# Two transformer layers in one kernel: when constants are loaded, early weights are split, and the first query tile's maxima are sent

## Chip, cores and metric

One core of one Trainium2 chip runs the whole program. The metric is device time in microseconds of one execution. The engines are called by the profile's short names as well: TensorE is PE (PEld is its weight load), VectorE is DVE, ScalarE is ACT, GpSimd is POOL, and SyncE, SP, only issues DMA transfers. "SPq" and "ACTq" are the sequencers that issue them.

## The reference

The input `x` has 2048 rows of 640 numbers in float32. Four blocks follow each other, and the two layers use the same weights:

```python
x = x + _A_ref(_layernorm(x, axis=-1), A_wqkv, A_wo)                # attention, 32 heads of 20
x = x + _B_ref(_layernorm(x, axis=-1), B_w1, B_b1, B_w2, B_b2)      # 640 -> 1536 -> 640
x = x + _A_ref(_layernorm(x, axis=-1), A_wqkv, A_wo)
x = x + _B_ref(_layernorm(x, axis=-1), B_w1, B_b1, B_w2, B_b2)
```

`_A_ref` multiplies by `wqkv`, takes `softmax(q k / sqrt(20)) v` over all 2048 keys in each head, and multiplies by `wo`. `_B_ref` is `relu(x w1 + b1)` squared, times `w2`, plus `b2`. The normalisation has no weights of its own.

## The kernel before

Products of activations and weights are made exact to about float32 from three products: each operand is split into a high part, rounded to the matmul's format, and a low part, the remainder (`split_to`: a cast on ScalarE, then a subtraction on VectorE; `split_on_pool`: a copy on ScalarE to a row buffer `r`, then cast and subtraction on GpSimd). Tiles of SBUF come from an arena of 42 slots and a ring of 11 row buffers; a tile that is dropped gives its place to a later one, which waits for the last reader.

Each layer has three stages. `qkv` makes queries, keys and values; `attention` makes scores, exponentials and sums; the rest is the output product and the two products of the dense block. The change lies in `qkv` and in what comes before it.

**Before `qkv`, first layer** (`begin_first`). Four row tiles of x (128 rows each) and four blocks of weight columns (`raw`, in the order `ORDER`) are fetched; two of the row tiles by ScalarE's queue, the rest by SyncE's. Each row tile gets its statistics (`stats`: VectorE, then two small GpSimd operations for the inverse deviation), is normalised and transposed on TensorE against the identity (line 1269), and the five transposed banks are split to `xnT`. The first two weight blocks are split between the third and the fourth row tile. After these instructions stand the constants: a row of ones that goes by `d_one` to `sums_t` and later to the keys, and the biases `b1_t` and `b2_t`. The program has one order per engine and per queue, the order in which it is written out.

**`qkv`.** Forty units (`UNITS`) come first, each a product of one block of 128 query or key columns (`pos`) with 512 rows (`tb`): positions 0 to 3 for each of the four row blocks, then positions 4 to 9. Then 32 chains of values follow (16 row tiles, two halves). The 128 rows of the contraction are cut in two halves of 64, `r` 0 and 1, which TensorE runs beside each other, one half a unit ahead of the other (`work_on`, `product`, line 320). A finished unit leaves PSUM in `end_qk` and is stored to `d_qk` (`later` keeps one store back). Between the products `insert` puts in the matmuls that find the largest score of each query (line 476, reduced on VectorE at line 488), as a small planner with costs for each engine allows; the tiles they need are loaded ahead in `tiles`, `load_q`, `load_k`, `load_kd`. `step_rest` advances normalising and transposing of the next rows (`front`, line 395). Two dictionaries, `early` and `late`, hold calls that run ahead of or behind a unit of a given number: fetches and splits of weights in the first layer; in the second, where split weights come back from DRAM, loads of `w_qk` and of the seven pieces of `w_v` (`wv<-d_wv`).

**The first query tile.** When all maxima of tile 0 are there, `end_group` reduces and transposes them (`mrows_max`, `mrows`), which GpSimd splits to `mr`, and writes them to DRAM (`d_m<-mr`); at the next insertion `mrows_load` reads them back as extra rows of the query tile (`q<-d_m`). The list `later_rows` joins the two. SyncE issues everything in order, and each of its transfers waits until its source is written.

Of the kernel before, what the change touches and what calls it, by code (L numbers as in the profile page):

```python
# [16 lines left out]
P = 128  # L17
# [4 lines left out]
DH = 20  # L22
# [17 lines left out]
def tile_layers(  # L40
# [249 lines left out]

    mark_t = cpool.tile([1, 2], F32, name="mark_t")
    nc.vector.memset(mark_t, 0.0)

    def after(later, earlier):
        tc.add_manual_dep(
# [32 lines left out]
    def end_qk(pos, tb, dst):  # L328
        ev = slot([P, 2, QB], F32R, "ev")
        which, jj = divmod(ORDER[pos], 5)  # L330
        rows = slice(jj * P, (jj + 1) * P)
        kd = None
        if which and pos < FIRST:


            if not keys:
                keys.update(of=slot([P, 2, QB], F32, "kf"), left=4)
            kf = keys["of"][:, jj, :]
            r = xtile("r")[:, :QB] if tb % 2 else kf
            if tb:  # L340
                split_on_pool(ev[:, 0, :], ev[:, 1, :], dst, r)
            else:
                split_to(ev[:, 0, :], ev[:, 1, :], dst)
                nc.scalar.copy(r, dst)
            if tb % 2:
                kd = slot([P, 2, QB], F32R, "kd")
                nc.gpsimd.tensor_sub(kf, r, kf)
                pool_hi(kd[:, 0, :], kf)
                pool_lo(kd[:, 1, :], kf, kd[:, 0, :].bitcast(F32))
            keys["left"] -= 1  # L350
            if not keys["left"]:
                keys.clear()
        else:
            (split_on_pool if tb or pos > 3 else split_to)(ev[:, 0, :], ev[:, 1, :], dst)

        def store():
            thrice(d_qk[which, tb, rows], ev, 1 + which)
            if kd is not None:
                thrice(d_kd[tb // 2, rows], kd, 2)

        return store
# [314 lines left out]
    def qkv(first, x_src, rest):  # L676
# [5 lines left out]
        state = {"n": 0, "turn": False, "op": None, "last": "one"}  # L682
        now = {"pe": 0.0, "dve": 0.0, "act": 0.0}
        busy = [0.0] * 8
        early, late, later_rows, soon = {}, {}, [], []
        coming = [y for x in DOUBLE for h in x for y in h if y[2] == "d"]

        def at(when, n, f):
            when.setdefault(n, []).append(f)

        for pos in range(2 if first else FIRST, 10):
            n = UNITS.index((0, pos)) - 5 if pos >= FIRST else pos - 2
            if first:
                if pos >= FIRST:
                    at(early, n - 2, lambda pos=pos: raws.append(raw_cols(wqkv, ORDER[pos])))
                at(late if n else early, n, lambda pos=pos: w_qk.put(
                    raws.pop(0), pos * 10, pos * 10 + KD, KD, nc.scalar.copy,
                    nc.vector.tensor_sub if pos == 2 else pool_lo,
                ))
            else:  # L700
                at(early, n, lambda pos=pos: w_qk.need(pos * 10, pos * 10 + 9))
        for k in range(KD if first else w_v.n):
            n = len(UNITS) - 7 + k
            if first:
                at(early, n - 2, lambda k=k: raws.append(raw_rows(wqkv[:, 2 * D :], k)))
                at(late, n, lambda k=k: w_v.put(
                    raws.pop(0), k * 4, k * 4 + 2, 2, nc.scalar.copy, pool_lo
                ))
            else:
                at(early, n, lambda k=k: w_v.load(k))  # L710
# [16 lines left out]
        def end_group(x):  # L727
            g, qb, c = x
            t = g * NQB + qb
            rest = soon + groups + double + [w[0] for w in work + twos] + [o["w"][0] for o in begun]  # L730
            if t == 0:
                left[t] -= 1 if c in range(4) else 2
                if left[t] == 0:
                    mrows_max(t)
                    mrows(t)
                    later_rows.append(t)
            if (t or left[t]) and all(y[:2] != (g, qb) for y in rest):
                del q_t[t]
            use = {(y[0], y[2]) for y in rest + coming}
            use |= {(h, 2 * "de".index(y)) for h, y in use if y not in range(4)}  # L740
            for y in [y for y in k_t if y[0] == g and y not in use]:
                if g < 2 or y[1] not in range(4):
                    del k_t[y]
# [59 lines left out]
        def insert(par):  # L803


            while later_rows:
                mrows_load(later_rows.pop())
            op = state["op"]
            if bool(op) != bool(par):
                return False  # L810
            if now["pe"] < max(busy[b] for b in ps_q.coming(1)):
                return False
            if state["turn"] and not par:
                if now["pe"] < max(busy[b] for b in ps_q.coming(2)):
                    return False
                now["pe"] += 1.2
                for spot in ps_q.coming(2):
                    takes("act", 0.6, spot)
                    takes("dve", 0.7, spot)
                step_rest()  # L820
                return False
            if not op:
                op = state["op"] = choose()
                if not op:
                    return False
                state["last"] = op["kind"]
            single(op, par)
            if par:
                state["op"] = None
            return True  # L830
# [10 lines left out]
        def end(n):  # L841

            what, a, b = chains[n]["of"]
            dst = chains[n].pop("dst")
            now["act"] = max(now["act"], now["pe"]) + 0.6
            if what == "qk":
                pending.append(end_qk(b, a, dst))
                if b >= FIRST and a == NQB - 1 or n == 4 * FIRST - 1:
                    w_qk.past(b * 10 + 9, w_qk.got)
                return  # L850
            f = end_v(a, b, dst)
            if f:
                later(1)
                pending.append(f)
                if a == 10:
                    load_v(0, 0)
                if a == 12:
                    for c in range(4):
                        assert (0, c) not in k_t
                        load_k(0, c, True)  # L860
                    load_q(1)
                if a == 14:
                    for c in (1, 3):
                        if (2, c) not in k_t:
                            load_k(2, c, True)
                if a % 4 == 3:
                    del xt_[a // 4]
# [374 lines left out]
    def second():  # L1242
# [7 lines left out]
            yield  # L1250
        yield from front(3, d_x[1], ps_q, 2, (1, 3))

    def begin_first():

        rows = []
        for i in range(4):
            t = xtile("x")
            dma((nc.sync, nc.scalar)[i % 2], t, x_in[i * P : (i + 1) * P, :])
            rows.append(t)
        for pos in range(FIRST):  # L1260
            raws.append(raw_cols(wqkv, ORDER[pos]))
        yield
        dsts = [ps_all("xt") for _ in range(KD)]
        mvs = []

        def turn(i):
            normalise(nc.vector if i else nc.gpsimd, rows[i], mvs[i])
            for k in range(KD):
                nc.tensor.transpose(
                    dsts[k][:, i * P : (i + 1) * P], rows[i][:, k * P : (k + 1) * P], ident  # L1270
                )

        for i in range(4):
            mvs.append(stats(rows[i]))
            if i:
                turn(i - 1)
        for pos in range(2):
            w_qk.put(raws.pop(0), pos * 10, pos * 10 + KD, KD, nc.scalar.copy, pool_lo)
        turn(3)
        rows.clear()  # L1280
        steps = [front(tb, x_in, ps_q, 2, (1, 3)[: tb - 1]) for tb in (1, 2, 3)]
        next(steps[0])
        res = []
        for k in range(KD):
            t = slot([P, 2, QB], F32R, "xnT")
            split_to(t[:, 0, :], t[:, 1, :], dsts[k])
            res.append(t)
            if k == KD - 1:
                xt_[0] = res
            yield 0, False  # L1290
        yield from fronts(steps)
# [1 line left out]
    b2_t = cpool.tile([P, D], F32, name="b2_t")  # L1293
    opening = begin_first()
    next(opening)
    ones = slot([2, QB], F32, "ones")
    nc.vector.memset(ones, 1.0)
    for p in range(2):
        dma(nc.scalar, d_one[:, p, :], ones)
    for h in range(4):  # L1300
        r = 32 * h + DH
        dma(nc.scalar, sums_t[r : r + 1, 32 * h : 32 * h + 32], d_one[0, :1, :32])
    dma(nc.sync, b1_t, b1.rearrange("(f p) -> p f", p=P))
    dma(nc.sync, b2_t, b2.partition_broadcast(P))
    ahead = second()
    layer(True, x_in, d_x[0], d_x[1], opening, ahead)
    layer(False, d_x[1], d_x[2], x_out, ahead, None)
# [28 lines left out]
```

## Time and profile before

| | |
|---|---|
| median of 3 runs | 3685.02 us (3682.33 to 3688.01) |
| the profiled execution | 3682.43 us |
| its span, first to last instruction | 3680.6 us |
| mean granted TensorE clock | 0.996 |
| PE busy | 3624.3 us (98%) |
| DVE, ACT, POOL busy | 2726.4, 2647.6, 804.9 us |

The profile comes from one execution. A timeline row gives start and duration in microseconds, engine, line of the kernel, operation, what it writes and reads, shapes, the number of instructions merged in it and, in brackets, the idle time of the engine before it with what ended it. A waits row gives total, number and longest. A windows row gives the stretch, then busy time and instructions of PE, PEld, DVE, ACT and POOL, the granted clock, and the share and rate of the DMA engines. A row of one tile or line gives shortest, median and longest duration in nanoseconds, first and last start, and shapes.

### The profile page before, as it was taken

How to read it: one execution, taken by the hardware profiler on the slowest of the kernel's cores; microseconds unless marked ns; L12 is line 12 of the kernel's file. 1: busy time of each engine (PE TensorE's matmuls, PEld its weight loads, DVE VectorE, ACT ScalarE, POOL GpSimd, SP SyncE). 2: the span in 40 equal slices, each digit the busy share in tenths (PEclk: the TensorE clock that was granted, in tenths of full speed). 3: DMA queues.
4: the chain of work that ended last, by engine and by line, in shares of the span. 5: the costliest groups of instructions: out<-in, count | busy, mean ns of one | idle time of the engine just before them, and what ended most of it. 6: DMA issues, size and time to landing. Idle time of an engine off the chain costs nothing.

```text
span 3680.6 us, 67584 instructions
## 1 busy us (share of the span) xinstructions
PE 3624.3 (98%) x25738; PEld 2161.0 (59%) x25738; DVE 2726.4 (74%) x5046; ACT 2647.6 (72%) x5202; POOL 804.9 (22%) x894
## 2 busy tenths in 40 slices
PE   7999999999999999999999899999999999999999
PEld 5897334334334336989878874334334333378998
DVE  6877999999999992344567679999999999723443
ACT  2678999999999994122227689999999999941221
POOL 4541344211211121111144202112211211201110
PEclk9999999999999999999999999999999999999999
DMA  7875555323211136411267643232232111373111
GB/s 231 284 251 167 163 145 165 111 65 76 61 46 47 50 100 224 174 44 44 100 225 248 205 148 88 61 81 60 67 79 55 50 49 44 109 251 137 43 49 38
DMA packets 255262, 426.51 MB, mean 116 GB/s; under 512 B 60445, under 2 KB 107293, under 8 KB 254937
## 3 DMA queue, kind: packets, MB, share of 16 engines
q1 hardware_dynamic: 254104, 419.82, 36.9%
q8 instruction: 202, 3.31, 0.4%
q10 hardware_dynamic: 832, 2.37, 0.2%
q14 instruction: 124, 1.01, 0.1%
HBM read 262.20 MB, written 159.88 MB: 115 GB/s over the span
## 4 chain that ended last, share of the span: by engine, by line
PE 94%; DVE 2%; DMA 2%; ACT 1%; SPq 0%; issue 0%; POOL 0%; ACTq 0%; DVEq 0%; POOLq 0%
PE banks L570 28%; PE banks L285 20%; PE banks L558 20%; PE banks L476 15%; PE banks L320 10%; DMA q<-d_qk 1%; DVE h L256 1%; PE banks L1122 0%; PE banks L395 0%; DVE r L1149 0%; ACT h L255 0%; DVE bst L243 0%; SPq L76 0%; ACT r L1148 0%; DVE x L251 0%
## 5 line engine op out<-in xcount | busy, mean ns | idle before, releaser
L565 ACT ACTIVATE e<-banks 128x512 f32<-128x512 f32 x4096 | 2113.3, 604 | 65.6 <-PE banks L476 5.4
L488 DVE TENSOR_REDUCE mx<-banks 128x1 f32<-128x512 f32 x3068 | 1925.8, 684 | 203.4 <-PE banks L476 130.9
L476 PE MATMUL banks<-k,q 60*128 60x512 f32 x3583 | 1245.1, 428 | 6.6 <-DMA q<-d_qk 4.8
L558 PE MATMUL banks<-q,k 62*128 62x512 f32 x4096 | 1152.9, 435 | 0.9 <-ACT rl L497 0.5
L570 PE MATMUL banks<-e,vg 128*32 128x512 f32 x8192 | 1092.8, 605 | 0.0
L558 PEld LDWEIGHTS banks<-q,k 62*128 62x128 f32 x4096 | 600.1, 185 | 695.0 <-ACT e L565 663.6
L476 PEld LDWEIGHTS banks<-k,q 60*128 60x128 f32 x3583 | 582.1, 185 | 293.3 <-DVE mx L488 217.4
L505 DVE CUSTOM_DVE_ANT_0 rl<-banks,rl 128x512 f32<-128x512 f32 x515 | 336.1, 689 | 116.3 <-PE banks L476 106.2
L320 PE MATMUL banks<-xnT,wqk 64*128 64x512 f32 x2400 | 388.4, 400 | 10.2 <-DVE ev L256 3.6
L570 PEld LDWEIGHTS banks<-e,vg 128*32 128x32 f32 x8192 | 161.6, 108 | 357.5 <-issue 332.9
L285 PE MATMUL banks<-w,h 128*128 128x320 f32 x2304 | 357.3, 312 | 5.7 <-DVE h L256 3.5
L285 PEld LDWEIGHTS banks<-w,h 128*128 128x128 f32 x2304 | 339.4, 188 | 15.2 <-DVE h L256 7.9
L497 ACT ACTIVATE rl<-banks 128x512 f32<-128x512 f32 x519 | 275.2, 597 | 98.3 <-PE banks L476 96.6
L285 PE MATMUL banks<-xnT,w 128*128 128x512 f32 x1440 | 330.0, 389 | 0.0
L1148 ACT ACTIVATE r<-banks,b_t 128x512 f32<-128x512 f32 x96 | 66.1, 689 | 359.5 <-PE banks L285 357.4
L320 PEld LDWEIGHTS banks<-xnT,wqk 64*128 64x128 f32 x2400 | 290.9, 190 | 45.1 <-DVE ev L256 4.4
L285 PEld LDWEIGHTS banks<-xnT,w 128*128 128x128 f32 x1440 | 269.5, 188 | 55.2
L267 POOL CAST mr<-nt 128x32 fp32r<-128x32 f32 x64 | 13.4, 209 | 1136.8 <-DVE nt L531 1103.2
L614 POOL TENSOR_TENSOR few<-few,minus_t 128x16 f32<-128x16 f32 x62 | 179.8, 2901 | 198.8 <-DMA few<-d_s 198.8
L320 PE MATMUL banks<-wv,xnT 64*128 64x320 f32 x1920 | 200.0, 308 | 12.0 <-DMA wv<-d_wv 10.1
L1168 DVE TENSOR_TENSOR x<-banks,x 128x320 f32<-128x320 f32 x128 | 62.9, 492 | 181.8 <-PE banks L285 180.1
L320 PEld LDWEIGHTS banks<-wv,xnT 64*128 64x128 f32 x1920 | 187.7, 186 | 14.2 <-DMA wv<-d_wv 10.6
(78 smaller groups left out, 1940.6 us busy)
## 6 DMA issues: line engine op xcount, KB each, us to landing
q<-d_qk SPq DMA_DIRECT2D x248, 240.0 KB
d_qk<-ev SPq DMA_DIRECT2D x80, 512.0 KB
k<-d_qk SPq DMA_DIRECT2D x152, 240.0 KB
x<-d_x SPq DMA_DIRECT2D x88, 320.0 KB
d_qk<-ev SPq DMA_DIRECT2D x80, 256.0 KB
d_o<-ot SPq DMA_DIRECT2D x248, 80.0 KB
ot<-d_o SPq DMA_DIRECT2D x38, 512.0 KB
d_v<-v SPq DMA_DIRECT2D x32, 512.0 KB
```

Of the source, the lines that this page charges most:

```text
L285: nc.tensor.matmul(dst, a, b, start=(n == 0), stop=(n == last))
L320: m = nc.tensor.matmul(ch["dst"][:, :width], *pair, start=first, stop=last)
L476: nc.tensor.matmul(dst, q_t[t][b : b + 60, p, sub * P : (sub + 1) * P], k_t[t // NQB, c][b : b + 60, p, :], start=True, stop=True,)
L488: nc.vector.tensor_reduce(maxima(t)[:, 2 * par + p, sub, c : c + 1], dst, axis=AX.X, op=ALU.max)
L497: nc.scalar.activation(res, dst, AF.Relu)
L505: nc.vector.tensor_tensor_reduce(out=r, in0=dst, in1=r, scale=1.0, scalar=LEAST, op0=ALU.add, op1=ALU.max, accum_out=maxima(t)[:, 2 * par ...
L558: nc.tensor.matmul(dst, k_t[t // NQB, kt // 4][b : b + 62, p, (kt % 4) * P : (kt % 4 + 1) * P], q_t[t][b : b + 62, p, :], start=True, stop ...
L565: nc.scalar.activation(es[p][:, par, :], dst, AF.Exp, scale=SCALE)
L570: nc.tensor.matmul(acc[32 * h : 32 * h + 32, :], v_t[t // NQB, kt // 8][:, kt % 8, 32 * h : 32 * h + 32], es[p][:, par, :], start=(kt == 0 ...
L614: nc.gpsimd.tensor_tensor(few, few, minus_t, op=ALU.pow)
L1148: nc.scalar.activation(r, dst, AF.Relu, bias=b1_t[:, f : f + 1])
L1168: nc.vector.tensor_add(x[:, c], dst[:, :HALF], x[:, c])
```

## The change

- The constants move from the start into a function `constants`, which runs ahead of unit 24 of the first layer; all their transfers are issued by SyncE, the first six of which ScalarE issued.
- A copy of one element on ScalarE stands right behind the setting of `mark_t`, ahead of the first transfers.
- The first row tile is normalised on VectorE, as the other three are. 24 transposes of the identity into a bank that nobody reads stand ahead of the rows' transposes, 8 behind them.
- The third and the fourth weight block are split ahead of unit 0 (the fourth was behind unit 1).
- In both layers the query and key units of positions 0 to 3 of the first 512 rows use `split_on_pool` as all others do; the second copy for the keys (line 344) is gone.
- Weights of the values are fetched and split (first layer) or loaded (second layer) one unit sooner.
- Tile 0's maxima are reduced and written at the fifth row tile of the values, and read back at the ninth.

```diff
     nc.vector.memset(mark_t, 0.0)
+    nc.scalar.copy(mark_t[:, 0:1], mark_t[:, 1:2])
...
-            if tb:
-                split_on_pool(ev[:, 0, :], ev[:, 1, :], dst, r)
-            else:
-                split_to(ev[:, 0, :], ev[:, 1, :], dst)
-                nc.scalar.copy(r, dst)
+            split_on_pool(ev[:, 0, :], ev[:, 1, :], dst, r)
...
-            (split_on_pool if tb or pos > 3 else split_to)(ev[:, 0, :], ev[:, 1, :], dst)
+            split_on_pool(ev[:, 0, :], ev[:, 1, :], dst)
...
+        if first:
+            at(early, 24, constants)
         for pos in range(2 if first else FIRST, 10):
-            n = UNITS.index((0, pos)) - 5 if pos >= FIRST else pos - 2
+            n = UNITS.index((0, pos)) - 5 if pos >= FIRST else 0
...
         for k in range(KD if first else w_v.n):
-            n = len(UNITS) - 7 + k
+            n = len(UNITS) - 8 + k
...
                 left[t] -= 1 if c in range(4) else 2
-                if left[t] == 0:
-                    mrows_max(t)
-                    mrows(t)
-                    later_rows.append(t)
...
-            while later_rows:
-                mrows_load(later_rows.pop())
...
                 pending.append(f)
+                if a == 4:
+                    assert left[0] == 0
+                    mrows_max(0)
+                    mrows(0)
+                if a == 8:
+                    mrows_load(0)
...
+    def constants():
+
+        ones = slot([2, QB], F32, "ones")
+        nc.vector.memset(ones, 1.0)
+        for p in range(2):
+            dma(nc.sync, d_one[:, p, :], ones)
+        for h in range(4):
+            r = 32 * h + DH
+            dma(nc.sync, sums_t[r : r + 1, 32 * h : 32 * h + 32], d_one[0, :1, :32])
+        dma(nc.sync, b1_t, b1.rearrange("(f p) -> p f", p=P))
+        dma(nc.sync, b2_t, b2.partition_broadcast(P))
...
+        def again(n):
+            for _ in range(n):
+                nc.tensor.transpose(banks[:, 7, :P], ident, ident)
+
+        again(24)
         def turn(i):
-            normalise(nc.vector if i else nc.gpsimd, rows[i], mvs[i])
+            normalise(nc.vector, rows[i], mvs[i])
...
         turn(3)
+        again(8)
```

More of the change, by code (lines that the diff above doesn't have):

```diff
@@ L684, in qkv @@
         busy = [0.0] * 8
-        early, late, later_rows, soon = {}, {}, [], []
+        early, late, soon = {}, {}, []
         coming = [y for x in DOUBLE for h in x for y in h if y[2] == "d"]
@@ L1263, in begin_first @@
         dsts = [ps_all("xt") for _ in range(KD)]
-        mvs = []
+        def again(n):
+            for _ in range(n):
+                nc.tensor.transpose(banks[:, 7, :P], ident, ident)
+        again(24)
         def turn(i):
-            normalise(nc.vector if i else nc.gpsimd, rows[i], mvs[i])
+            normalise(nc.vector, rows[i], mvs[i])
             for k in range(KD):
@@ L1271, in turn @@
                 )
+        mvs = []
         for i in range(4):
@@ L1295, in tile_layers @@
     next(opening)
[L1296 to L1304, printed above, removed]
     ahead = second()
```

## The prediction

> **What bounds the kernel now.** I read the chain that ended last, then the waits of the whole run by engine, then the timelines around the largest waits. The chain is TensorE's almost alone:
>
> ```profile
> PE 94%; DVE 2%; DMA 2%; ACT 1%; SPq 0%; issue 0%; POOL 0%; ACTq 0%; DVEq 0%; POOLq 0%
> ```
>
> So an edit pays only where it takes away idle or slow time of TensorE. Its waits over the run (us in total, times, longest):
>
> ```profile
> core 0 of [0], span 3680.6 us
> engine line waited for: us in total, times, longest us
> PE banks L1269 <- POOL x L251: 10.3, 1, 10.3
> PE banks L320 <- DMA wv<-d_wv: 10.1, 1, 10.1
> PE banks L476 <- DMA q<-d_qk: 6.9, 5, 2.0
> PE banks L395 <- DVE x L251: 4.6, 8, 1.8
> PE banks L320 <- DVE ev L256: 3.6, 2, 2.3
> ```
>
> The reader is to see two single waits of ten microseconds, the start and one load of value weights; nothing else comes near. The profiled execution took 3682.43 us, 1.8 of them outside the span; it lies 2.6 below the median, 3685.02. The sum is made against the execution, and the difference is then put on the median.
>
> **The wait for the value weights, in the second layer.** SyncE's queue (start, duration), TensorE where it goes on, and a window of the same time with the granted clock:
>
> ```profile
> 2046.11 0.78 SPq L76 DMA_DIRECT2D wv<-d_wv  x1
> 2052.88 1.16 SPq L76 DMA_DIRECT2D d_m<-mr  x2
> 2056.35 0.57 SPq L76 DMA_DIRECT2D q<-d_m  x2
> ...
> 2060.61 0.92 SPq L76 DMA_DIRECT2D wv<-d_wv  x1
> ```
>
> ```profile
> 2067.96 0.63 PE L320 MATMUL banks<-wv,xnT 64*128 64x320 f32 x1 [10.14 <-DMA wv<-d_wv]
> ```
>
> ```profile
> 2067.96:2072.00 4.04, 4.04 (x27) 3.92 (x28) 0.70 (x2) 2.25 (x5) 1.90 (x2) 0.61 0.64 217
> ```
>
> The last piece of `wv` goes out at 2060.61 and TensorE stands until 2067.96. Ahead of it in the queue stand the two writes of `d_m`, which wait for the maxima (until 2052.88), and the two reads, which wait for the writes to land (until 2056.35). The change sends both pairs from inside the value chains (at the fifth and ninth row tile) and each `wv` one unit sooner. The last piece then takes the place that the last but one has now, 2046.1. At the 7.35 us that it took now (2060.61 to 2067.96) it lands by 2053.5, and the products reach it at 2067.96 - 10.14 = 2057.8: the wait goes. Of the 4.04 us after it the clock was at its low state, 0.50 (a window further down is wholly in it), for (1 - 0.61) x 4.04 / 0.5 = 3.2 us: another 1.6. This term is -11.7. What is late next: the loads that stood behind `d_m` also go about ten microseconds sooner, so nothing in the trace. The same writes in the value chains hold the queue for the 3.5 us from 2052.88 to 2056.35 at most, spread over two places, behind stores that no product waits for: 0.
>
> **The start, first layer.** ScalarE, then GpSimd, VectorE and TensorE:
>
> ```profile
> 11.77 1.28 ACT L159 ACT_TABLE_LOAD   x1 [11.77 <-DMA sums_t<-d_one]
> 13.07 1.35 ACT L159 CAST wqk<-raw 128x640 fp32r<-128x640 f32 x2
> 14.32 1.06 ACT L255 CAST xnT<-banks 128x512 fp32r<-128x512 f32 x2
> ```
>
> ```profile
> 7.77 2.50 POOL L251 TENSOR_SCALAR x<-x,mv 128x640 f32<-128x640 f32 x1
> ```
>
> ```profile
> 12.17 0.61 DVE L251 TENSOR_SCALAR x<-x,mv 128x640 f32<-128x640 f32 x1 [0.44 <-POOL mv L247]
> ```
>
> ```profile
> 10.33 4.53 PE L1269 MATMUL banks<-ident,x 128*128 128x128 f32 x20 [10.33 <-POOL x L251]
> 18.07 6.05 PE L320 MATMUL banks<-xnT,wqk 64*128 64x512 f32 x30 [3.21 <-DVE xnT L256]
> 24.62 3.69 PE L320 MATMUL banks<-xnT,wqk 64*128 64x512 f32 x30 [0.50 <-ACT mark_t L322]
> 30.72 0.49 PE L320 MATMUL banks<-xnT,wqk 64*128 64x512 f32 x2 [2.40 <-ACT wqk L159]
> ```
>
> ```profile
> 40.16 1.20 PE L320 MATMUL banks<-xnT,wqk 64*128 64x512 f32 x4 [2.26 <-DVE ev L256]
> ```
>
> Four steps. (1) The first row is normalised on VectorE (0.61) and not on GpSimd (2.50), so the transposes no longer pile up behind 10.33. I let the table load and the small copy, now first on ScalarE, delay the two rows of x that it sends by 1.4 us (1.28 and a copy of one element), and still have the last row normalised by about 12.0 (12.78 now) and the first split at 12.7 instead of 14.32: -1.6. Weights are split before that, since ScalarE's queue is free of constants. (2) The fourth weight block is split ahead of unit 0 and not after unit 1: the 2.40 at 30.72 goes. (3) The key and query blocks of the first 512 rows leave PSUM by one copy on ScalarE; VectorE's subtraction, which stood behind statistics, is out of the way. Of the 2.26 at 40.16 about 0.65 is left (a copy of 0.57 to 0.59 and its signal): -1.6. (4) The pause before 40.16 had cost the clock:
>
> ```profile
> 40.16:45.00 4.84, 4.84 (x28) 3.93 (x30) 1.95 (x5) 0.00 (x0) 1.53 (x3) 0.65 0.83 252
> ```
>
> (1 - 0.65) x 4.84 / 0.5 = 3.4 us at half speed, so -1.7. With some 0.6 of short waits for rows behind the same subtraction, TensorE would come to its first maxima 7.9 us sooner.
>
> But the queries are not there then. The low and high parts now come from GpSimd, and SyncE is in order behind the store of the second block:
>
> ```profile
> 49.18 0.61 POOL L267 CAST xnT<-r 128x512 fp32r<-128x512 f32 x1 [6.64 <-ACT r L262]
> 49.88 1.30 POOL L270 TENSOR_TENSOR xnT<-r,xnT 128x512 fp32r<-128x512 f32 x1
> ```
>
> ```profile
> 40.13 0.88 SPq L76 DMA_DIRECT2D d_qk<-ev  x2
> 41.06 1.51 SPq L76 DMA_DIRECT2D x<-in_A_x_dram  x2
> ```
>
> ```profile
> 49.37 0.92 SPq L76 DMA_DIRECT2D q<-d_qk  x2
> ```
>
> ```profile
> 56.84 0.29 PEld L476 LDWEIGHTS banks<-k,q 60*128 60x128 f32 x3 [0.47 <-DVE mv L244]
> ```
>
> The row of 56.84 is the first use of `q`, sent at 49.37: it comes just in time now. In the new order the block closes 4.0 sooner (steps 1 and 2), but its split waits for three rows' variances on GpSimd and then takes 0.61 + 1.30: the store and all loads behind it, rows of x, keys, queries, come only about 2.0 sooner. TensorE waits some 5.9 us there, a wait that takes the place of those removed: -2.0 is left. Behind it, VectorE catches up during that wait, so the pauses before the last rows' transposes shrink to nothing:
>
> ```profile
> PE banks L395 <- DVE x L251: 3.4, 3, 1.8
> ```
>
> ```profile
> 65.00:70.00 5.00, 5.00 (x23) 3.60 (x23) 1.39 (x2) 2.34 (x4) 2.49 (x3) 0.50 0.95 286
> ```
>
> That is -3.4 (the answer for 56 to 72 us), and the half-speed stretch around 65 to 70 moves to the new wait, about -0.5. The start gives -5.9 in all; bounds -9.6 (no new wait, 7.9 and half of the 3.4) and 0 (the loads come no sooner, the pauses stay).
>
> **The second layer's start** has the same blocks. The smaller of the two `ev` waits, 3.6 - 2.3 = 1.3, shrinks to 0.65, but queries are waited for already (five times in the run, 6.9 us). Their loads stand behind a store that comes later by GpSimd's 0.61 + 1.30 less a subtraction as long as the normalising of a row, 0.61, so by 1.3, of which 0.65 is won back: about +0.6, from -0.65 to +1.3; I take +0.5.
>
> **Constants at unit 24.** They stand in SyncE's queue near 150 us, one vector fill of `ones` with them on VectorE. Now they hold ScalarE until 11.77, and SyncE:
>
> ```profile
> 6.18 3.89 SPq L76 DMA_DIRECT2D b_t<-in_B_b_dram  x2
> ```
>
> So in SyncE's queue 11.77 + 3.89 = 15.7 us at most in which no load follows. Against it, TensorE is full there and SyncE spends much of its time waiting for data to store (windows and queue waits, 150 to 200 and 150 to 260 us):
>
> ```profile
> 150.00:200.00 50.00, 50.00 (x424) 40.74 (x422) 39.73 (x123) 38.32 (x84) 24.17 (x27) 1.00 0.76 257
> ```
>
> ```profile
> SPq L76 <- POOL ev L270: 27.4, 13, 4.1
> ```
>
> I take 0, nearest to those rows; if the loads ahead (two groups) did not cover it, up to +15.7. A gain is excluded, since TensorE has no idle time there.
>
> **The transposes of the identity.** 24 before the rows and 8 behind them. At the present pace of 20 in 4.53 us they take 5.4 and 1.8 us, inside waits of 10.33 and 3.21: 0 if they do nothing else. Whether they raise the clock is the one thing to weigh:
>
> ```profile
> L1269 PE MATMUL banks<-ident,x x20: 421/421/476, 10.3 to 14.4; 128*128 128x128 f32 x20
> ```
>
> The 20 transposes of the start have a median equal to their least, 421 ns, so none ran faster than the first ones; and the 30 products behind them took 6.05 us against 3.69 for the next 30. So 4.53 us of transposes raised nothing, and I take 0. [...]
>
> **Sum.** -11.7 - 5.9 + 0.5 + 0 = -17.1: 3665.3 for a run like the profiled one, 3667.9 on the median.
>
> **Rivals.** *The clock rises by the transposes*: the first products run in 3.69 and not 6.05, another -2.4: 3665.5. For it only that 5.4 us is longer than any stretch of transposes seen. *No new wait for queries*: GpSimd is free sooner than I think, the start gives -9.6: 3664.2. *The start gives nothing*: the wait for queries eats all and VectorE's pauses stay; -11.7 + 0.5: 3673.8. *The change doesn't remove the wait for `wv`*: it takes no slot until another tile lets go, so only the start counts: 3679.6, no difference. *Slower*: with each value weight split one unit sooner, its slot of the arena may not be free yet, and ScalarE, in order, stands at each of the five casts of the first layer:
>
> ```profile
> L159 ACT CAST wv<-raw x6: 453/722/731, 202.8 to 222.6; 128x640 fp32r<-128x640 f32 x4, 128x320 fp32r<-128x320 f32 x2
> ```
>
> If a slot is let go a whole unit later ((222.6 - 202.8) / 4 = 4.95 us from cast to cast; one block takes two), the five cost 24.8: -17.1 + 24.8 = +7.7, 3692.7. It decides from a slot that is freed 17.1 / 5 = 3.4 us after it is asked for. Against it, the casts come at the even pace of the units now, so no slot was late for any of them.
>
> **How the numbers follow.** A run of this kernel can be told from no change from about 0.2%, 7.4 us. Forecast 0.55 (faster); clock 0.10, no new wait 0.13, start nothing 0.11 (all faster); wait stays 0.06 (same); slower 0.05. A little of the faster cases lies under 7.4 us if constants cost something: faster 0.87, same 0.07, slower 0.06. The range goes from the best start with a raised clock (3664.2 - 2.4) and the 2.7 to 3.0 us that single runs lie from their median (3682.33, 3688.01), 3658, to the last wait kept or constants that cost 11 on top of the forecast, 3679.
>
> **What would show it.** Right: no TensorE wait for `wv`; the first split before 13 us; first products still 6 us for 30; a TensorE wait of 4 to 7 us for `q` near 48 us; `constants` in SyncE's queue near 145 to 160 us with TensorE full. Wrong: a wait for `wv` above 2 us, or any TensorE idle time between 100 and 320 us.

## The result, and the profile after

The changed kernel takes 3667.69 us in the median of 4 runs (3665.23 to 3667.85), the kernel before 3685.6 (3682.33 to 3688.01, 4 runs): a ratio of 0.995, 95% interval 0.9933 to 0.9968. The forecast was 3667.9. The profiled execution took 3667.64 us, with a span of 3665.0; before it was 3682.43 and 3680.6. So 14.8 us of difference are to be found in the two traces.

The chain that ended last is still TensorE's, to 95%. Two of TensorE's waits (total, number, longest, in us); the first is now its largest:

```profile
PE banks L473 <- DMA q<-d_qk: 11.1, 4, 4.1
...
PE banks L392 <- DVE x L251: 1.7, 3, 1.0
```

Both waits of ten microseconds are gone, the start's and that for `wv`. The queries have taken the first place: 11.1 us, where it was 6.9. VectorE's pauses ahead of transposes, 4.6 before, are 1.7.

The start after, as timelines of TensorE (start, duration, idle time before in brackets), ScalarE, VectorE and GpSimd:

```profile
1.36 4.47 PE L1278 MATMUL banks<-ident 128*128 128x128 f32 x24 [1.36 <-POOL ident masks.py:199]
...
15.83 3.71 PE L321 MATMUL banks<-xnT,wqk 64*128 64x512 f32 x30 [1.24 <-DVE xnT L256]
20.11 4.15 PE L321 MATMUL banks<-xnT,wqk 64*128 64x512 f32 x34 [0.56 <-ACT mark_t L323]
...
31.30 4.60 PE L321 MATMUL banks<-xnT,wqk 64*128 64x512 f32 x37 [0.58 <-ACT r L262]
...
50.59 1.94 PE L473 MATMUL banks<-k,q 60*128 60x512 f32 x4 [4.08 <-DMA q<-d_qk]
```

```profile
0.73 1.28 ACT L293 ACT_TABLE_LOAD   x1 [0.73 <-PEq L1330]
1.07 0.89 ACTq L76 DMA_DIRECT2D x<-in_A_x_dram  x2
...
12.07 2.54 ACT L255 CAST xnT<-banks 128x512 fp32r<-128x512 f32 x5 [2.76 <-PE banks L1284]
```

```profile
10.24 1.27 DVE L251 TENSOR_SCALAR x<-x,mv 128x640 f32<-128x640 f32 x1 [0.71 <-POOL mv L247]
...
10.17 3.58 POOL L270 TENSOR_TENSOR wqk<-raw,wqk 128x384 fp32r<-128x384 f32 x4
```

Set against the rows of before: TensorE leads by 2.24 us at the first products (18.07 to 15.83), by 4.5 at the next (24.62 to 20.11), and by 8.9 where the wait for `ev` stood (40.16 to 31.30). The first maxima then wait 4.08 us for `q`; before they ran at 56.41, so 5.8 is left. After that the pauses before the last transposes are gone. The lead at four later places is read from the start of the first scores, two points of the second layer and the end of its values (before, then after):

```profile
56.41 1.16 PE L476 MATMUL banks<-k,q 60*128 60x512 f32 x4
331.64 1.22 PE L558 MATMUL banks<-q,k 62*128 62x512 f32 x4 [0.54 <-ACT rl L497]
1870.63 1.66 PE L320 MATMUL banks<-xnT,wqk 64*128 64x512 f32 x12 [1.31 <-DVE ev L256]
2166.94 0.85 PE L320 MATMUL banks<-wv,xnT 64*128 64x320 f32 x8 [1.35 <-ACT mark_t L322]
```

```profile
321.57 1.22 PE L555 MATMUL banks<-q,k 62*128 62x512 f32 x4 [0.53 <-ACT rl L494]
1861.55 3.69 PE L321 MATMUL banks<-xnT,wqk 64*128 64x512 f32 x30 [0.58 <-ACT r L262]
1875.19 1.78 PE L473 MATMUL banks<-k,q 60*128 60x512 f32 x4 [3.15 <-DMA q<-d_qk]
...
2148.96 0.85 PE L321 MATMUL banks<-wv,xnT 64*128 64x320 f32 x8 [1.35 <-ACT mark_t L323]
```

The lead is 10.1 us at the first scores, 9.1 in the second layer's products and 18.0 behind the values. Between the last two stands the wait for `wv`. The lead just ahead of it is read from SyncE's queue, from the last store ahead of the loads of `kd`, `k` and `q` (before, then after):

```profile
2045.26 0.79 SPq L76 DMA_DIRECT2D d_qk<-ev  x2
```

```profile
2039.11 0.80 SPq L76 DMA_DIRECT2D d_qk<-ev  x2
2039.96 1.75 SPq L76 DMA_DIRECT2D wv<-d_wv  x1
```

It is 6.2 us. The last load of `wv` now goes out right behind this store, and 18.0 - 6.2 = 11.8 us were won at its wait. On the way there 9.1 - 6.2 = 2.9 were lost, between 1861 and 2040 us. Windows of that stretch, before and then after (PE, PEld, DVE, ACT, POOL busy, granted clock, DMA share, GB/s):

```profile
1870.00:1925.00 55.00, 48.41 (x385) 41.09 (x385) 36.37 (x61) 8.88 (x23) 21.36 (x22) 0.97 0.86 270
```

```profile
1870.00:1925.00 55.00, 48.48 (x365) 41.06 (x365) 40.83 (x71) 9.81 (x26) 26.87 (x28) 0.91 0.92 300
```

By the clock's loss, (0.97 - 0.91) x 55 = 3.3 us more than before went to low clock. It comes with longer waits for `q`, 3.15 in the row above and 3.29 near 1896 us, where the longest was 2.0 before: about their ends the granted clock goes to 0.50, from 1875.2 to 1878.7 and from 1899.1 to 1906.0 (before, in this stretch, from 1883.4 to 1886.8 alone). Of the lead of 18.0 another 2.4 had gone at the end (spans: 15.6). Of these, 1.7 are a stretch of 3.4 us at half clock right behind the values, from 2155.14 on, which the trace of before does not have there. The rest was not followed up; single runs of one version differ by as much.

### The profile page after: what moved, and what is told of

The parts are those of the page before. It is cut to its first block, busy times and chain, and to the rows that moved or that the text cites. A ratio compares the mean times of both kernels' runs of the same rounds, so it can differ in the third digit from the quotient of the medians.

```text
span 3665.0 us, 67658 instructions
## 1 busy us (share of the span) xinstructions
PE 3627.8 (99%) x25770; PEld 2165.3 (59%) x25770; DVE 2725.3 (74%) x5039; ACT 2645.5 (72%) x5199; POOL 819.1 (22%) x909
## 4 chain that ended last, share of the span: by engine, by line
PE 95%; DVE 2%; ACT 1%; DMA 1%; POOL 1%; issue 0%; SPq 0%; ACTq 0%; DVEq 0%; POOLq 0%
PE banks L567 28%; PE banks L285 21%; PE banks L555 20%; PE banks L473 16%; PE banks L321 10%; DMA q<-d_qk 1%; DVE h L256 1%; PE banks L1121 0%; DVE r L1148 0%; ACT h L255 0%; PE banks L392 0%; DVE mx L485 0%; ACT r L1147 0%; DVE bst L243 0%; SPq L76 0%
## 5 line engine op out<-in xcount | busy, mean ns | idle before, releaser
L255 ACT CAST xnT<-banks 128x512 fp32r<-128x512 f32 x70 | 39.9, 588 | 212.9 <-PE banks L1121 132.0
```

## The experiments

The labels are the names under which the expectations went on record. The medians of before were 3683.73, 3684.5 and 3685.3 us in the three groups of four; each ratio is to the group's own. They and the 3685.6 above differ by up to 1.9 us, so a difference of that size between runs of different groups says nothing.

**1. No transposes of the identity** (`e1_no_identity`)

```diff
-        again(24)
-        again(8)
```

> The changed kernel without the 24 and the 8 transposes of the identity; nothing else differs. Theory A (these transposes raise the clock before the rows come): the first 30 products take about 6.0 us again and not 3.71, the four groups of row transposes run at half clock, all of it costs 2.4 to 3.0 us: about 3670.3 against 3667.7. Rival B (the clock rose because the row transposes now stand closer together, the identity adds nothing): the first 30 products stay near 3.7 us and the time at 3667.7.

Measured: 3667.01 us (3666.76 to 3667.54), ratio 0.9955 (0.9942 to 0.9967).

```profile
15.85 6.04 PE L321 MATMUL banks<-xnT,wqk 64*128 64x512 f32 x30 [2.94 <-DVE xnT L256]
...
53.91 1.87 PE L473 MATMUL banks<-k,q 60*128 60x512 f32 x4 [5.12 <-DMA q<-d_qk]
```

The mechanism is theory A's: without the transposes the same 30 products, begun at the same time, take 6.04 us and not 3.71. Each row's five transposes take 1.33 us here, as long as the one group of the changed kernel that ran at a granted clock of 0.50 (at 11.56 us); its other three take 0.77. (The profile's granted clock reads 1.00 under the 6.04 us, as it does under the 6.05 of before: that the clock was low there is read from the durations alone.) The first maxima come 3.3 us later, and of that 3.0 are left behind the values (2151.92 against 2148.96). The time, however, does not show it: at the end of the two spans only 0.6 is left, most of the rest having gone to the half clock at 2155.14, which this trace does not have. The raised clock was worth 2.3 us in these 30 products (6.04 - 3.71), and the half clock of 2155.14 alone took 1.7 of them back.

**2. The old way out of PSUM for the first 512 rows** (`e2_old_split`)

```diff
-            split_on_pool(ev[:, 0, :], ev[:, 1, :], dst, r)
+            if tb:
+                split_on_pool(ev[:, 0, :], ev[:, 1, :], dst, r)
+            else:
+                split_to(ev[:, 0, :], ev[:, 1, :], dst)
+                nc.scalar.copy(r, dst)
...
-            split_on_pool(ev[:, 0, :], ev[:, 1, :], dst)
+            (split_on_pool if tb or pos > 3 else split_to)(ev[:, 0, :], ev[:, 1, :], dst)
```

> The changed kernel with the old way out of PSUM for positions 0 to 3 of the first 512 rows (cast on ScalarE, subtraction on VectorE) in both layers. Theory A (the new TensorE wait for q near 46.5 us comes from GpSimd's splits, which hold the stores and so the loads in SyncE's queue): the wait of 4.08 falls below 1.5 us, the second layer's 3.15 to about 2; the waits for ev come back (about 2.3 and 1.3 us), and the half clock after 49 us is shorter; the sum is between -3 and +1: 3664.7 to 3668.7. Rival B (the rows of x, 1.3 MB ahead of q in the queues, make it late, not the splits): the wait for q stays within 1 us of 4.08, the ev waits come on top: about 3671.

Measured: 3667.66 us (3664.98 to 3671.63), ratio 0.9959 (0.9946 to 0.9971).

```profile
PE banks L396 <- DVE x L251: 5.8, 9, 1.9
...
PE banks L321 <- DVE ev L256: 3.5, 2, 2.2
```

Theory A. The first layer's wait for `q` at 46.5 us is gone (0.67 near 92 us is left), so it did come from GpSimd's splits. In the second layer the 3.15 became 1.66 and 0.30, but the later wait stayed (3.41, after the change 3.29). The `ev` waits (3.5) and VectorE's pauses (5.8, after the change 1.7) are back. This part of the change trades one loss for another, and the time is the changed kernel's.

**3. The two edits at the values alone, on the kernel before** (`e3_values_only`)

```diff
-            n = len(UNITS) - 7 + k
+            n = len(UNITS) - 8 + k
...
+                if a == 4:
+                    mrows_max(0)
+                    mrows(0)
+                if a == 8:
+                    mrows_load(0)
```

(and the calls in `end_group` and `insert` taken out)

> The kernel before with two edits alone: the weights of the values one unit sooner, and tile 0's maxima sent at the fifth and read back at the ninth row tile of the values. Theory A (the 10.14 us wait for the last wv in the second layer stood behind the d_m transfers, and 1.6 us of low clock behind it): the wait goes, 11.7 less than before: 3673.9. Rival B (most of it comes back as other waits, or as low clock elsewhere, since the stretches at half clock were seen to appear in other places): 3677 to 3681. The start up to 100 us is as before in both.

Measured: 3673.8 us (3668.51 to 3675.32), ratio 0.9972 (0.996 to 0.9983). Its waits begin as those of before, without `wv`:

```profile
PE banks L1269 <- POOL x L251: 10.2, 1, 10.2
PE banks L476 <- DMA q<-d_qk: 6.0, 3, 2.3
```

Theory A, 3673.9. Against this group's before, 3683.73, it is 9.9 and not 11.7; the 95% interval, 6.3 to 14.7 us, holds both. The rest of the change is then worth 3673.8 - 3667.7 = 6.1 us.

**4. The first group of maxima one unit later** (`e4_first_group_later`)

```diff
+                if n == 4:
+                    have.extend(PLAIN[0][0])
+                    soon[:] = [y for y in soon if y not in PLAIN[0][0]]
+                if n == 3:
+                    pass
-                if step % 2:
+                elif step % 2:
```

> The changed kernel with the first group of maxima opened one unit later (about 3.7 us); its loads stay where they are. Theory A (the 4.08 us wait for q near 46.5 us, the 6.83 us at half clock behind it and the second layer's 3.15 us with 3.4 at half clock are pure loss): the waits fall below 1 us each, 4.08 + 3.4 + 3.15 + 1.7 less, about 12: 3656. Rival B (VectorE falls behind, so that the transposes of the last 512 rows wait for normalised rows as in the kernel before): pauses of 3.4 us come back in the first layer, and the gain is 3 to 6: 3662 to 3665.

Measured: 3656.15 us (3652.21 to 3657.1), ratio 0.9924 (0.991 to 0.9937).

```profile
PE banks L473 <- DMA q<-d_qk: 4.0, 3, 2.8
PE banks L392 <- DVE x L251: 3.1, 5, 1.0
```

Theory A. That it is met to 0.2 us is luck: a wait of 2.81 at 82.27 us is new, the first 30 products took 5.30 us and not 3.71, and the second layer's later wait, 3.29, went too, which A had not counted. The loads stay where they were and TensorE has products to do while they land; VectorE's pauses grow only from 1.7 to 3.1. The new wait was a loss in itself and not the cover of another.

**5. Maxima the old way, weights one unit sooner** (`e5_old_maxima`): `end_group` and `insert` as in the kernel before, the two calls at the fifth and ninth row tile out.

> The changed kernel with tile 0's maxima sent and read back the old way, right behind their last group; the weights of the values stay one unit sooner. Theory A (it is enough that the last wv is issued ahead of the d_m transfers): it goes out near 2040 us as in the changed kernel, TensorE waits for no wv, 3667.7. Rival B (the d_m pair alone was the cause, wherever wv stands): a wait for wv or for the loads behind it of 5 to 10 us comes back: 3673 to 3678.

Measured: 3664.84 us (3664.21 to 3668.18), ratio 0.9948 (0.9935 to 0.996). SyncE's queue:

```profile
2037.42 2.32 SPq L76 DMA_DIRECT2D wv<-d_wv  x1
2044.19 1.16 SPq L76 DMA_DIRECT2D d_m<-mr  x2
```

Theory A: the last `wv` goes out 6.8 us ahead of the `d_m` pair, and no wait for it is in the trace. Moving the maxima adds nothing that can be measured.

**6. Maxima moved, weights at their old units** (`e6_wv_later`)

```diff
-            n = len(UNITS) - 8 + k
+            n = len(UNITS) - 7 + k
```

> The changed kernel with the weights of the values at their old units; the maxima stay in the value chains. Theory A (moving the maxima is enough): the last wv goes out near 2045 to 2047 us instead of 2039.96, lands 7 us later, and TensorE waits for it 2 us at most: 3667.7 to 3669.5. Rival B (both edits are needed, since the loads of kd, k and q stand ahead of it as well): a wait for wv of 4 to 8 us: 3672 to 3677.

Measured: 3670.8 us (3669.83 to 3672.42), ratio 0.9963 (0.9951 to 0.9976).

```profile
PE banks L321 <- DMA wv<-d_wv: 3.3, 1, 3.3
```

```profile
2048.82 0.33 SPq L76 DMA_DIRECT2D wv<-d_wv  x1
```

Between the theories: with `d_m` gone from ahead of it, the load still stands behind `kd`, `k`, `q` and a store, and TensorE waits 3.3 us. `d_m` made about seven of the ten microseconds, the place of the load the other three; the earlier place alone removes both.

**7. Constants at the start** (`e7_constants_first`): the lines of `constants` back behind `next(opening)`, the first six transfers on ScalarE's queue.

> The changed kernel with the constants back at the start, the first six transfers on ScalarE's queue. Theory A (they held ScalarE's first cast): the first weights are cast at about 11.8 us or later and not at 7.5, the first split is at 14.3 and not at 12.07, the first products come 2.2 us later, and the time rises by 2 to 3: 3670.0. Rival B (the wait for q near 46.5 us absorbs it, since the loads stand behind GpSimd's splits and not behind TensorE): the wait for q shrinks by about 2 us, first maxima near 50.6 as before: 3667.7.

Measured: 3664.71 us (3660.54 to 3665.99), ratio 0.9944 (0.9932 to 0.9957). ScalarE, VectorE, GpSimd, TensorE:

```profile
7.46 2.49 ACTq L76 DMA_DIRECT2D sums_t<-d_one  x4
9.99 1.35 ACT L159 CAST wqk<-raw 128x640 fp32r<-128x640 f32 x2 [7.78 <-DMA raw<-in_A_wqkv_dram]
...
10.13 0.61 DVE L251 TENSOR_SCALAR x<-x,mv 128x640 f32<-128x640 f32 x1 [0.71 <-POOL mv L247]
...
10.79 3.35 POOL L270 TENSOR_TENSOR wqk<-raw,wqk 128x384 fp32r<-128x384 f32 x4 [0.70 <-ACT wqk L159]
...
15.00 3.69 PE L321 MATMUL banks<-xnT,wqk 64*128 64x512 f32 x30 [2.56 <-DVE xnT L256]
```

Neither theory: the first products come 0.8 us sooner than with the constants moved. The view puts ScalarE's wait ahead of its first cast down to `raw`, but the constants' last four transfers hold its queue from 7.46 to 9.95, and the cast follows at 9.99. In the kernel before it came at 13.07: the four transfers held the queue until 11.74 there, and the table load stood behind them. The changed kernel casts at 7.46 already, and the later cast is better: GpSimd's subtraction then starts behind the last row's normalising, which takes 0.61 us. In the changed kernel the two overlap, and it takes 1.27. Moving the constants was worth nothing, at most a small loss.

**8. The first pair of key tiles later as well** (`e8_first_two_later`): as run 4, and

```diff
-            if n in (10, 13, 17):
+            if n in (11, 13, 17):
```

> The changed kernel with the first group of maxima opened one unit later, as in the run before (3656.15), and the first pair of key tiles (the ones that are added before the maximum) one unit later too. Theory A (the 2.81 us wait for q at 82.27 us, 1.7 at half clock behind it and the 0.90 at 1904 go): 3651. Rival B (the pair's own loads go later with it, so the wait only moves): 3656.

Measured: 3653.1 us (3650.81 to 3654.58), ratio 0.9912 (0.9899 to 0.9926).

```profile
PE banks L473 <- DMA q<-d_qk: 0.5, 1, 0.5
```

The wait for `q` is 0.5 us in the whole run, and the median is 3.1 below run 4's, between the theories and nearer A; the two intervals overlap. Beside the changed kernel it is 14.6 us less.

**9. The fourth weight block split behind unit 1** (`e9_old_weight_units`)

```diff
-            n = UNITS.index((0, pos)) - 5 if pos >= FIRST else 0
+            n = UNITS.index((0, pos)) - 5 if pos >= FIRST else pos - 2
```

> The changed kernel with the fourth weight block split behind unit 1 again. Theory A (the start is paced by the loads of q, so a wait ahead of it only moves): a wait of about 2.4 us for wqk comes back near 24 to 28 us, and the wait for q at 46.5 us, 4.08 now, shrinks by as much; first maxima near 50.6: 3667.7, at most 1 more. Rival B (the early split is worth its 2.4 us and the low clock behind it): first maxima 2.4 us later, 3670 to 3672.

Measured: 3670.08 us (3665.72 to 3672.36), ratio 0.996 (0.9946 to 0.9973).

```profile
24.69 0.73 PE L321 MATMUL banks<-xnT,wqk 64*128 64x512 f32 x4 [1.06 <-ACT wqk L159]
27.03 0.51 PE L321 MATMUL banks<-xnT,wqk 64*128 64x512 f32 x2 [0.58 <-POOL wqk L270]
...
52.73 1.86 PE L473 MATMUL banks<-k,q 60*128 60x512 f32 x4 [4.46 <-DMA q<-d_qk]
```

The wait back is 1.6 us, less than the 2.4 of before, and the wait for `q` does not shrink: the loads of `q` go later with the products whose results they fetch. The first maxima come 2.1 us later. That speaks for B; the times alone do not settle it.

**10. The first row normalised on GpSimd** (`e10_first_row_gpsimd`)

```diff
-            normalise(nc.vector, rows[i], mvs[i])
+            normalise(nc.vector if i else nc.gpsimd, rows[i], mvs[i])
```

> The changed kernel with the first row tile normalised on GpSimd again (2.50 us there). Theory A (the four variances and the splits of weights stand behind it on GpSimd, so all of the start is later): the first split comes at about 14 us and not at 12.07, the first products about 2 us later, and the loads of q with them: 3669.7. Rival B (absorbed by the wait for q): first maxima near 50.6 us, 3667.7.

Measured: 3666.84 us (3665.82 to 3669.27), ratio 0.9953 (0.994 to 0.9965).

```profile
16.68 3.69 PE L321 MATMUL banks<-xnT,wqk 64*128 64x512 f32 x30 [2.48 <-DVE xnT L256]
...
51.43 2.07 PE L473 MATMUL banks<-k,q 60*128 60x512 f32 x4 [4.12 <-DMA q<-d_qk]
```

The first products come 0.85 us later and the first maxima 0.84, less than half of what A said; the time does not show it. The wait for `q` absorbs nothing here either.

**11 and 12. The fastest version with the constants at the start, and with 16 transposes behind the rows** (`e11_later_constants_first`, `e12_more_identity`): run 8 with the edit of run 7; then `again(16)` for `again(8)`.

> The version with the first group and the first pair of key tiles opened one unit later (3653.1), with the constants at the start. Theory A (with the constants there, the weights' casts and with them GpSimd's subtraction come later than the last row's normalising, which then takes 0.61 us and not 1.27: first products at 15.0 and not 15.6 to 15.8): 0.7 to 2 us less, 3651 to 3652.4. Rival B (the difference of the run with the constants at the start was chance): 3653.1 or more.

> As the run before it in this call, with 16 and not 8 transposes of the identity behind the rows. Theory A (the idle 2.5 us before the first products lets the clock fall for one window of 3.4 us in about half of the runs; more work in it keeps the clock up): no half clock between 14 and 20.5 us, first 30 products 3.7 us in the profile, the median 0.8 to 1.7 less than that run. Rival B (the clock's windows are set elsewhere, or the extra transposes run into the products): the same or up to 1 more.

Measured: 3653.1 us (3649.78 to 3656.05), ratio 0.9914 (0.99 to 0.9927), and 3653.94 (3650.65 to 3657.29), ratio 0.9916 (0.9903 to 0.993). A window of the second, up to 15.38 us, where its clock goes to half for 3.42 us:

```profile
11.97:15.38 3.41, 1.27 (x12) 1.03 (x10) 2.75 (x5) 3.41 (x9) 2.95 (x4) 1.00 0.97 272
```

Rival B both times. What run 7 won at the start is not seen here: the constants' transfers hold ScalarE's queue until 10.41 us this time and not 9.95, and the first products come at 15.47, where run 8 had 15.58. The extra transposes, run at a granted clock of 1.00, end at 13.24 us: TensorE works 1.27 of the 3.41 us and then idles, and the first products begin at half clock (0.50 from 15.38 on; 5.11 us for the 30).

## Why the prediction was right, point by point

**The wait for `wv`: -11.7.** Right in place and size in the traces (18.0 of lead behind it, 6.2 ahead of it, so 11.8); 9.9 between medians in run 3. The cause was told in part only. Of the three edits that it credits together, the earlier load alone does it (run 5); with `d_m` gone but the load at its old unit, 3.3 us would have stayed (run 6).

**The start: -5.9.** The lead at the first scores is 10.1, past the bound of -9.6, in the profiled pair; with the second layer's loss it is 6.1 between the medians of run 3 and the changed kernel, where -5.9 + 0.5 was said. By steps:

- (1) The first split came at 12.07, not 12.7. The step that failed is the 1.4 us allowed for the table load: the two rows of x went out at 1.07, inside that load (0.73 to 2.01). What did hold the last row was not foreseen: VectorE's normalising beside GpSimd's subtraction, 1.27 for 0.61 (run 7). The first row on VectorE is worth 0.85 (run 10).
- (2) The 2.40 wait went, as said; put back, it is 1.6 (run 9).
- (3) 0.58 is left of 2.26, where 0.65 was said.
- (4) The low clock after 40.16 went (the granted clock reads 1.00 from 14.98 to 49.12). But the clock did rise with the transposes, which is the rival that had 0.10: 3.71 us for the first 30 products, and 6.04 without them (run 1). The step that failed is the inference from the 4.53 us of transposes in the kernel before, behind which the products did take 6.05, to 24 of them from 1.36 us on. These took 4.47 us, where 5.4 was worked out for the old pace: the first 16 of them 3.39 us (0.21 each), the last 8 the other 1.08 (0.14 each), so the clock rose under them, as the durations have it; the granted clock reads 1.00 throughout. Why the 4.53 us had raised nothing no run here tried.
- The new wait for `q` was right in kind and cause (run 2), 4.08 at 46.5 us where 5.9 near 48 was said. The stretch at half clock moved to it, as said (49.12 to 55.95). The store of the second block went out at 35.33, behind the three variances and the split on GpSimd, as the working had it; the rows of x, keys and queries follow it:

```profile
33.20 0.61 POOL L267 CAST ev<-r 128x512 fp32r<-128x512 f32 x1
...
35.33 0.88 SPq L76 DMA_DIRECT2D d_qk<-ev  x2
36.30 2.54 SPq L76 DMA_DIRECT2D x<-in_A_x_dram  x4
...
42.95 1.61 SPq L76 DMA_DIRECT2D q<-d_qk  x2
```

The term that was mis-sized is "only about 2.0 sooner": the store went out 4.8 sooner (40.13 before) and `q` 6.4 (49.37 before). The block had closed 7.2 sooner and not 4.0 (ScalarE reads it at 30.68, before at 37.86), 2.3 of it by the clock; the way through GpSimd took 2.4 of that back, near the 2.0 of the working. TensorE, in turn, came to its first maxima 9.9 sooner and not 7.9. One reading under this term is wrong as well: the row of 56.84 does not show that `q` came just in time in the kernel before. The first use was the matmul of 56.41, and the 0.47 ahead of the row was a wait for VectorE.

**The second layer: +0.5.** The lead fell from 9.1 to 6.2, a loss of 2.9 between those points, past the upper bound of +1.3. Left out was the clock: from the ends of the waits of 3.15 and 3.29 us on it was at 0.50 for 3.4 and 6.8 us, where it had been for 3.4 in all, and that lost 3.3 us more than before.

**Constants: 0.** Right to half a microsecond, and their old place was as good (run 7). In SyncE's queue they stand at 142.78, where 145 to 160 was said. But TensorE was not quite full there: right behind VectorE's fill of `ones` (0.48 us, at 142.27) it waits 0.45 us for VectorE. The prediction had called any idle time of TensorE between 100 and 320 us a sign of being wrong, and by that this step failed. The wait stands in all nine traces with the constants at unit 24 (0.27 to 0.46 us) and in none of the five with them at the start.

The total came out right to 0.2 us by luck, because the errors cancel: a start that gained more than said (the clock, a smaller wait), a second layer that gave back more, and low clock in other places.

## What to carry to other kernels

When a load is late in an in-order queue, look at what stands ahead of it and try its place alone first; here one unit sooner did alone what was done with three edits. When a change frees an engine, follow what it frees into the next queue: the new wait for `q` was the largest loss left, and it went by opening its consumers one unit later, with nothing loaded sooner. Gains of 1 to 3 us that a trace shows near the start need not be found in the time, when the clock loses as much elsewhere (run 1: 3.3 us at the first maxima, 0.6 between the spans).

## What the runs showed of the hardware that was not expected

The granted clock went in steps of 3.41 us. In the changed kernel's trace the half clock begins and ends at 11.57, 14.98, 49.12 and 55.95, all whole steps apart:

```profile
11.57:14.98 3.41, 3.03 (x13) 2.62 (x13) 2.29 (x4) 2.90 (x6) 2.18 (x3) 0.50 0.76 220
...
45.71:49.12 3.41, 0.81 (x8) 0.34 (x4) 1.66 (x6) 0.67 (x2) 3.17 (x7) 1.00 1.03 300
49.12:52.53 3.41, 1.94 (x7) 1.37 (x9) 1.08 (x2) 0.00 (x0) 3.27 (x5) 0.50 0.95 325
52.53:55.95 3.42, 3.42 (x20) 2.87 (x18) 3.33 (x6) 0.00 (x0) 1.85 (x2) 0.50 0.65 259
```

In these rows a step follows the one before it: behind 0.81 us of work in 3.41 the clock is at half, behind 1.94 still at half, behind 3.03 and 3.42 (the work at half clock) full again. The busy time does not decide it alone, though. In the same trace the half clock of 2155.14 follows this step, which is busy almost throughout:

```profile
2151.73:2155.14 3.41, 3.26 (x15) 1.36 (x11) 1.69 (x4) 3.21 (x8) 0.00 (x0) 1.00 0.39 157
```

Where the steps fall differs from run to run (in run 12 the half clock began at 15.38, behind a step with 1.27 us of work), and what a wait costs in clock differs too: in the changed kernel 3.4 us at half came with the wait of 3.15, and 6.8 with the wait of 3.29. In run 4's trace the first products took 5.30 us behind an idle 2.48:

```profile
15.55 5.30 PE L321 MATMUL banks<-xnT,wqk 64*128 64x512 f32 x30 [2.48 <-DVE xnT L256]
```

In run 10, behind the same 2.48 us, they took 3.69. So the same products took 3.71, 5.30 or 6.04 us. Of eight traces with the transposes of the identity four have them at 3.69 to 3.71 us (the changed kernel, runs 7, 9 and 10) and four at 5.11 to 5.30 (runs 2, 4, 11 and 12): the 2.3 us of run 1 are the good case. From which share of work the clock rises was not tried.

The other surprise is the last row's normalising, 1.27 us beside GpSimd's subtraction and 0.61 where that starts later (run 7). In the changed kernel's trace the subtraction starts at 10.17 and the normalising of 1.27 us at 10.24; in run 7's the normalising starts at 10.13 and the subtraction at 10.79. Why the one takes longer beside the other is not shown; no run tried it alone.
